# Where a unit's spread softmax shift is written: the bank of the preceding unit's column sums instead of spare columns of its PV banks

## The chip, the cores and the metric

The kernel runs on one core of a Trainium2 chip. The metric is the time of one execution on the device in microseconds, as the median of several runs; lower is better. Besides the timed runs there is one execution that the hardware profiler recorded. The engines are PE (matrix products), DVE (vector), ACT (scalar functions), POOL (GpSimd) and SP, which here only issues transfers. Matrix products are written to eight PSUM banks, each 512 float32 wide on 128 partitions; everything else is in SBUF.

## The reference, cut to what matters

Attention with normalised q and k, and behind it a two-layer product with a leaky ReLU:

```python
# q, k, v: (8, 12, 448, 64)
q_n, k_n = rmsnorm(q, g_q), rmsnorm(k, g_k)
scores = q_n @ k_n.transpose(0, 1, 3, 2) / sqrt(64)
attn = exp(scores - scores.max(-1)); attn = attn / attn.sum(-1)
x = (attn @ v).transpose(0, 2, 1, 3).reshape(8 * 448, 768)
h = x @ w_in                    # (3584, 2048)
out = maximum(0.01 * h, h) @ w_out   # (3584, 768)
```

The softmax needs no exact row maximum. Any shift that is the same for all keys of a row leaves the result as it is, as long as the exponentials stay in range. The kernel uses one shift for a whole unit.

## The kernel before, in words

**Units.** A unit is four heads of one batch: 3 units for each of 8 batches, 24 in all, u = 0 to 23. The four heads lie as two (r) on the halves of the partitions and two (a) in the two banks of a pair. The 448 tokens are 7 steps of 64.

**One unit.** `load` brings q and k in (SP's queue), two units to four ahead. `prep_sq` (ACT), `prep_ssq` (DVE, L186), `prep_rinv` (ACT) and `prep_norm` (DVE, L198) normalise them into `n16`; `prep_trd` transposes it by a transfer, and `prep_g` (DVE, L182) puts the gains on q. `score` (PE, L228) makes the transposed scores of one step in a pair of banks, and `ex` (ACT, L243) takes their exponential, `et`, with the unit's shift `eb` as bias. `pv` (PE, L400) multiplies with v over all 7 steps into two PV banks. `zcol` (PE, L337) makes the column sums of the exponentials in the first 224 columns of one more bank, `zc`.

**The shift.** `shift_max` takes the maximum over the scores of step 0 for each partition (DVE, L257) and puts the 128 values on the diagonal of a matrix, `dg` (L259). `shift_mm` brings them to all partitions: ones times `dg` on PE (L271), the maximum along the row (DVE, L274), and `eb` = 1 minus that (L284). Each PV bank has 64 spare columns behind its 448, and the product is written there in two halves, for units 4 to 23. Units 1 and 2 use spare columns of their own score banks, units 0 and 3 a free bank (L279).

**Copy and division.** `pv_out` copies the two PV banks to SBUF, `x32` (DVE at L350 for units 3 to 6, ACT at L352 for units 7 to 22), and `drop` gives the banks back. `zcol_ln` (ACT, L358) takes the logarithm of the sums and gives their bank back, `zcol_inv` (L363) takes exp of minus that, and four transfers (SP's queue, L368) spread the result over the partitions as `rz`. `xmul_pool` multiplies `x32` and `rz` into `xt` (L378): on POOL for units 7, 8, 11, 13, 14, 17, 19, 20 and 21, on DVE for the others (`xmul_sb`).

**The order.** All of it is written out by hand. The loop goes over u = 3 to 23 and four quarters d. For a narrow unit (`narrow`: u = 3 to 22) quarter 0 of the next one is recorded as follows:

```python
qk(u, (0,)); shift_max(u); flush()
pv_slot(u - 1); zcol(u - 1); shift_mm(u); pv_out(u - 1)
ex(u, 2); zcol_ln(u - 1)
```

Each engine works through its instructions in this order; semaphores make it wait where data or a bank require it. Waits are put in by the framework from the regions that instructions touch. `zcol_inv` follows as a job of quarter 0, `xmul_pool` in quarter 1. From u = 5 on (`tripled`) the score steps are recorded as 0, then 1 to 3 in quarter 1, then 4 to 6 in quarter 3.

**What lies between.** `fill` takes pieces of the two-layer product from `queue`, as many for each quarter as the strings of `PLAN` say, and puts a job behind each. `moe1` is the first layer (PE, L422; leaky ReLU on ACT, L416). The second layer is `moe2` (L468) and `seven` (L521), which makes a block product out of seven smaller ones: DVE makes sums of blocks of `gt` in `sa` (`s1` to `s4`: L502, L505, L508, L511), PE multiplies, and DVE adds the results to an output tile (L528, L543). Work that DVE or ACT does on a piece's result is put off by `later` until `flush`. The last two batches have the first layer in seven products too (`late1`, L655).

**Banks.** `aux` hands out a single bank and `slot` a pair, the one that has been free for longest within the rules; `drop` gives back. `banks` is one tile, so that all products have the name `banks` in the profile.

Of the kernel before, what the change touches and what calls it, by code (L numbers as in the profile page):

```python
# [8 lines left out]
FP32 = mybir.dt.float32  # L9
FP16 = mybir.dt.float16  # L10
AF = mybir.ActivationFunctionType
ALU = mybir.AluOpType
AXL = mybir.AxisListType
# [5 lines left out]
def kernel(  # L19
# [11 lines left out]
    nc = tc.nc  # L31

    B, H, S, D = q.shape
    QH = 4
    NS = 7
    P = 128
# [11 lines left out]
    small = ctx.enter_context(tc.tile_pool(name="small", bufs=2))  # L48
# [39 lines left out]
    def drop(tile_):  # L88
        for i in range(8):
            if tile_ is single[i]:  # L90
                assert i not in free
                free.append(i)
                return
        x = [i for i in range(4) if tile_ is double[i]][0]
        assert 2 * x not in free and 2 * x + 1 not in free
        free.extend((2 * x, 2 * x + 1))
# [9 lines left out]
    onesp = cst.tile([P, P], FP16)  # L106
# [32 lines left out]
    st = {}  # L139
# [121 lines left out]
    def shift_bank(u):  # L261
        st[u]["pb"] = aux()

    def shift_mm(u):
        s = st[u]
        peak = s["spare"][:, 510:511]
        own = s.get("own")
        if own is not None or u > 0 and "pslot" in st[u - 1]:
            pb = (st[u - 1]["pslot"] if own is None else own)[:, :, S:S + 64]
            for x in range(2):  # L270
                nc.tensor.matmul(pb[:, x], onesp, s["dg"][:, 64 * x:64 * x + 64], start=True, stop=True)  # L271
            if own is not None:
                peak = small.tile([P, 1], FP32, tag="peak", name="peak")
            nc.vector.tensor_reduce(peak, pb, axis=AXL.XY, op=ALU.max)  # L274
        else:
            if "pb" not in s:
                shift_bank(u)
            pb = s["pb"]
            nc.tensor.matmul(pb[:, 0:P], onesp, s["dg"], start=True, stop=True)  # L279
            nc.vector.tensor_reduce(peak, pb[:, 0:P], axis=AXL.X, op=ALU.max)  # L280
            if u >= 3:
                drop(pb)
        s["eb"] = small.tile([P, 1], FP32, tag="eb", name="eb")
        nc.vector.tensor_scalar(s["eb"], peak, -1.0, DELTA, op0=ALU.mult, op1=ALU.add)  # L284
# [550 lines left out]
    with tc.manual_schedule():  # L835
# [54 lines left out]
        shift_bank(0)  # L890
        warm(18, st[0]["pb"])
        shift_mm(0)
        drop(st[0]["pb"])
        prep_ssq(1)
# [47 lines left out]
        warm(4, wb)  # L942
        drop(wb)
        shift_mm(1)
        prep_ssq(2)
        ex(1)
# [29 lines left out]
        ex(1)  # L976
        warm_edge(16, st[0]["pv"][1])
        shift_mm(2)
        qk(1, (6,))
        ex(1)  # L980
# [203 lines left out]
```

## Time and profile before

| what | value |
|---|---|
| median of 3 runs | 409.88 us (409.75 to 410.16) |
| profiled execution | 409.67 us, its span 407.9 us |
| PE busy | 396.9 us, 97% of the span |
| DVE, ACT, POOL busy | 307.1, 300.6, 72.9 us |
| matmul of the shift, L271 | 44 instructions, 128x64, the first at 19.4 us, the last at 347.9 us |
| maximum over it, L274 | 22 instructions, 20 of them for units 4 to 23, 300 ns each (median) |
| copy of the PV banks by ACT, L352 | 16 instructions, 905 ns each (median) |

The profiled execution took 409.67 us, of which 407.9 us lie between its first and its last instruction. Times within it are counted from the first instruction. A line such as L352 is a line of the kernel before. Engine and letter q (SPq) mean that the engine's sequencer issued a transfer or waited. PE's matmuls are pipelined: they start closer together than they last, so distances are read from start to start.

### The profile page before, as it was taken

The numbers are of one execution on the slowest core, as the hardware profiler recorded it, in microseconds if no ns is written. First come the engines' busy times: TensorE is split into PE (matmuls) and PEld (weight loads), VectorE is DVE, ScalarE is ACT, GpSimd is POOL, SyncE is SP. The second block draws the span as 40 slices with busy tenths as digits, with TensorE's granted clock in tenths as the row PEclk, the third lists the DMA queues.
The fourth block names the chain that finished last, engine by engine and source line by source line (L and its number), as shares of the span: only waits on it lengthen the run. The fifth ranks groups of instructions, "written<-read, shape, count | busy, mean of one in ns | idle before, by whom it ended". The sixth has DMA issues, their size and how long they took to land.

```text
span 407.9 us, 9571 instructions
## 1 busy us (share of the span) xinstructions
PE 396.9 (97%) x3896; PEld 224.9 (55%) x3896; DVE 307.1 (75%) x481; ACT 300.6 (74%) x474; POOL 72.9 (18%) x86
## 2 busy tenths in 40 slices
PE   8999999999999999999999999999999999999996
PEld 7665454544455544555455544554455557559963
DVE  5887999959879665867679766777579888567672
ACT  5998877787978599778878689867996667743600
POOL 1887431200020200020021200021011202000000
PEclk9999999999999999999999999999999999999999
DMA  6999999898664984677664894776752560022023
GB/s 199 277 240 249 240 234 248 212 189 185 164 159 85 251 227 73 178 198 163 164 145 78 230 223 103 195 181 142 170 100 47 124 151 18 16 71 79 2 55 99
DMA packets 72526, 62.87 MB, mean 154 GB/s; under 512 B 36388, under 2 KB 67620, under 8 KB 72484
## 3 DMA queue, kind: packets, MB, share of 16 engines
q1 hardware_dynamic: 61888, 50.08, 46.8%
q0 software_dynamic: 10272, 11.80, 18.4%
q8 instruction: 30, 0.49, 0.5%
q10 hardware_dynamic: 324, 0.39, 0.3%
q14 instruction: 12, 0.10, 0.1%
HBM read 45.61 MB, written 11.01 MB: 139 GB/s over the span
## 4 chain that ended last, share of the span: by engine, by line
PE 80%; ACT 3%; DVE 3%; issue 2%; DMA 1%; SPq 1%; ACTq 0%; DVEq 0%
PE banks L422 27%; PE banks L521 23%; PE banks L228 8%; PE banks L655 6%; PE banks L400 6%; PE banks L468 6%; PE banks L337 3%; ACT et L243 1%; DMA rq<-in_q_dram 1%; SPq L368 1%; PE banks L271 1%; ACT gt L416 1%; DVE banks L257 1%; ACT sq L175 0%; PE banks L210 0%
## 5 line engine op out<-in xcount | busy, mean ns | idle before, releaser
L243 ACT ACTIVATE et<-banks,eb 128x896 f16<-128x896 f32 x168 | 161.4, 1015 | 28.9 <-PE banks L228 18.3
L422 PE MATMUL banks<-xt,win 128*128 128x448 f16 x612 | 122.4, 353 | 1.0 <-DVE xt L378 1.0
L422 PEld LDWEIGHTS <-win 128*128 128x128 f16 x612 | 57.3, 98 | 57.2 <-issue 8.0
L416 ACT ACTIVATE gt<-banks 128x448 f16<-128x448 f32 x104 | 56.4, 563 | 5.1 <-PE banks L422 3.9
L186 DVE TENSOR_REDUCE ssq<-sq 128x14 f32<-128x896 f32 (+2 forms) x49 | 50.3, 1057 | 0.7 <-ACT sq L175 0.7
L228 PE MATMUL banks<-qkT 64*64 64x448 f16 x672 | 49.3, 361 | 1.5 <-DVE qkT L810 0.8
L521 PEld LDWEIGHTS <-sa 128*128 128x128 f16 x352 | 33.4, 98 | 24.6 <-issue 3.6
L521 PE MATMUL banks<-tw,sa 128*128 128x384 f16 x264 | 46.9, 326 | 0.1
L528 DVE TENSOR_TENSOR ost<-banks,ost 128x384 f32<-128x384 f32 x55 | 30.4, 552 | 16.3 <-PE banks L521 14.3
L257 DVE TENSOR_REDUCE banks<-banks 128x1 f32<-128x896 f32 x24 | 26.3, 1097 | 14.2 <-PE banks L228 10.6
L400 PE MATMUL banks<-et,vt 64*64 64x448 f16 x672 | 36.9, 349 | 0.0
L521 PEld LDWEIGHTS <-gt 128*128 128x128 f16 x264 | 25.5, 98 | 18.7 <-issue 2.2
L468 PE MATMUL banks<-wout,gt 128*128 128x384 f16 x192 | 33.7, 327 | 0.0
L198 DVE TENSOR_TENSOR n<-rq,rinv 128x896 f16<-128x896 f32 (+2 forms) x25 | 31.0, 1241 | 3.1 <-ACT rinv L192 3.1
L228 PEld LDWEIGHTS <-qkT 64*64 64x64 f16 x672 | 16.9, 105 | 29.5 <-issue 22.5
L521 PE MATMUL banks<-wout,gt 128*128 128x384 f16 x176 | 32.4, 327 | 0.0
L290 POOL COPY gate_t<-qkT 128x1 f16<-128x1 f16 x16 | 4.8, 299 | 153.5 <-DMA qkT<-n 153.5
L378 POOL TENSOR_TENSOR xt<-x,rz 128x896 f16<-128x896 f32 x9 | 19.0, 2109 | 72.7 <-DMA rz<-zs 67.0
L352 ACT COPY x<-banks 128x896 f32<-128x896 f32 x16 | 14.5, 906 | 21.5 <-DVE banks L274 21.5
L198 DVE TENSOR_TENSOR n<-rk,rinv 128x896 f16<-128x896 f32 (+2 forms) x26 | 26.1, 1011 | 0.0
L400 PEld LDWEIGHTS <-vt 64*64 64x64 f16 x672 | 20.0, 107 | 10.0
L468 PEld LDWEIGHTS <-gt 128*128 128x128 f16 x192 | 17.8, 98 | 13.7 <-issue 2.9
(106 smaller groups left out, 484.7 us busy)
## 6 DMA issues: line engine op xcount, KB each, us to landing
rq<-in_q_dram SPq DMA_DIRECT2D x24, 448.0 KB, 4.8
rk<-in_k_dram SPq DMA_DIRECT2D x24, 448.0 KB, 5.3
out_dram<-ost SPq DMA_DIRECT2D x52, 192.0 KB, 3.4
rz<-zs SPq DMA_DIRECT2D x80, 112.0 KB, 2.8
vt<-in_v_dram POOLq DMA_DIRECT2D x24, 224.0 KB, 4.5
win<-in_moe_w_in_dram POOLq DMA_DIRECT2D x8, 384.0 KB, 14.9
wout<-in_moe_w_out_dram POOLq DMA_DIRECT2D x2, 1536.0 KB, 28.6
out_dram<-ost SPq DMA_DIRECT2D x4, 96.0 KB, 2.1
```

The costliest lines, as they stand in the source:

```text
L186: nc.vector.tensor_reduce(buf(u, "ssq")[:, ti, :, c[0]:c[1]], buf(u, f"sq{ti}")[:, :, c[0]:c[1]], axis=AXL.X, op=ALU.add)
L198: nc.vector.tensor_tensor(buf(u, "n16")[:, ti, c[0]:c[1]].rearrange("p s a d -> p a s d"), src[:, :, c[0]:c[1]], buf(u, "rinv")[:, ti, :, ...
L228: nc.tensor.matmul(banks[a][64 * r:64 * r + 64, 0:S].rearrange("p (t x) -> p t x", t=NS), kT(u, r, a, t), qT(u, r, a), start=True, stop=True)
L243: nc.scalar.activation(s["et"][:, t], sT[:, :, 0:S], AF.Exp, bias=s["eb"], scale=1.0)
L257: nc.vector.tensor_reduce(s["spare"][:, 511:512], sT[:, :, 0:S], axis=AXL.XY, op=ALU.max)
L400: nc.tensor.matmul(s["pv"][r][64 * a:64 * a + 64, 0:S], vts[u % NV][64 * r:64 * r + 64, a, t], s["et"][64 * r:64 * r + 64, t, a], start=(t ...
L416: nc.scalar.activation(dst, src, AF.Prelu, bias=0.0, scale=1.0, alpha=0.01)
L422: nc.tensor.matmul(hps[:, 0:S], win16[:, kt // 2, kt % 2, ts(ft, P)], xt[:, kt // 2, kt % 2], start=(kt == 0), stop=(kt == KT - 1))
L468: nc.tensor.matmul(op2[:, 0:HC], gt[:, ft, ds(col(t), P)], wout16[:, ft, ds(HC * half, HC)], start=(i == 0), stop=(i == FT - 1))
L521: nc.tensor.matmul(bank[:, 0:HC], a[:, f], b[:, f], start=(first and f == 0), stop=(f == HF - 1), skip_group_check=not first)
L528: nc.vector.tensor_tensor(dst, g[name][:, 0:HC], src, op=ALU.add)
L655: nc.tensor.matmul(bank[:, HX * i:HX * i + HX].rearrange("p (t x) -> p t x", t=NS), w, x[:, kt], start=start, stop=(kt == HK - 1), skip_gr ...
```

## The change

For units 4 to 23 the product of ones and `dg` is written in one piece of 128 columns into the bank `zc` of the preceding unit, at columns 256 to 383, behind the column sums in columns 0 to 223. Before, it was written in two pieces of 64 columns into the spare columns of the two PV banks of that unit. The maximum reads the new place. Units 0 to 3 keep their places. Nothing else is edited; lines behind the edit move by 3.

```diff
         own = s.get("own")
-        if own is not None or u > 0 and "pslot" in st[u - 1]:
-            pb = (st[u - 1]["pslot"] if own is None else own)[:, :, S:S + 64]
+        if own is not None:
+            pb = own[:, :, S:S + 64]
             for x in range(2):
                 nc.tensor.matmul(pb[:, x], onesp, s["dg"][:, 64 * x:64 * x + 64], start=True, stop=True)
-            if own is not None:
-                peak = small.tile([P, 1], FP32, tag="peak", name="peak")
+            peak = small.tile([P, 1], FP32, tag="peak", name="peak")
             nc.vector.tensor_reduce(peak, pb, axis=AXL.XY, op=ALU.max)
+        elif u > 0 and "zc" in st[u - 1]:
+            pb = st[u - 1]["zc"][:, 2 * P:3 * P]
+            nc.tensor.matmul(pb, onesp, s["dg"], start=True, stop=True)
+            nc.vector.tensor_reduce(peak, pb, axis=AXL.X, op=ALU.max)
         else:
```

## The prediction

> **What bounds the kernel now.** I read the busy shares first, then the waits, then the chain of work and the timeline around the places it pointed to. The page says that PE is the wall:
>
> ```profile
> PE 396.9 (97%) x3896; PEld 224.9 (55%) x3896; DVE 307.1 (75%) x481; ACT 300.6 (74%) x474; POOL 72.9 (18%) x86
> PE 80%; ACT 3%; DVE 3%; issue 2%; DMA 1%; SPq 1%; ACTq 0%; DVEq 0%
> ```
>
> The granted clock is 9 tenths or more in every slice. So the time can only change by what PE executes and by the moments at which PE waits. Among the waits one belongs to the lines of this change:
>
> ```profile
> ACT x L352 <- DVE banks L274: 21.5, 13, 3.3
> ```
>
> ACT's copy of the PV result (L352, 16 units) waits 21.5 us in all, 13 times, for the maximum over the spread shift (L274) that DVE takes from the same two banks. ACT is not the wall, so this is no sum to subtract; it says who will run earlier. I looked for what that sets going in unit 20's first half, around the copy for unit 19 (timeline: start, us, engine, line, operation, count; in brackets the idle time ahead):
>
> ```profile
> 297.37 3.57 PE L422 MATMUL banks<-xt,win 128*128 128x448 f16 x18
> 298.01 0.91 ACT L352 COPY x<-banks 128x896 f32<-128x896 f32 x1 [0.72 <-DVE banks L274]
> 298.01 0.16 DVE L284 TENSOR_SCALAR eb<-banks 128x1 f32<-128x1 f32 x1
> 298.81 1.01 ACT L243 ACTIVATE et<-banks,eb 128x896 f16<-128x896 f32 x1
> 300.37 0.41 ACT L363 ACTIVATE zs<-zs 128x224 f32<-128x224 f32 x1
> 300.80 2.48 SPq L368 DMA_DIRECT2D rz<-zs  x4
> 304.63 0.42 DVE L502 TENSOR_TENSOR sa<-gt 128x512 f16<-128x512 f16 x1 [0.17 <-ACT gt L416]
> 305.09 0.42 DVE L505 TENSOR_TENSOR sa<-sa,gt 128x512 f16<-128x512 f16 x1
> 305.14 2.32 POOL L378 TENSOR_TENSOR xt<-x,rz 128x896 f16<-128x896 f32 x1 [6.04 <-DMA rz<-zs]
> 305.16 1.46 PE L521 MATMUL banks<-tw,sa 128*128 128x384 f16 x8
> 305.90 1.84 DVE L508 TENSOR_TENSOR sa<-gt 128x512 f16<-128x512 f16 x1
> 308.00 0.55 DVE L528 TENSOR_TENSOR ost<-banks,ost 128x384 f32<-128x384 f32 x1
> ```
>
> Read it downwards: copy, exponential, reciprocal of the sums (L363), four broadcasting DMAs, POOL's product (L378). And read L508: the same shape takes 0.42 us elsewhere, here 1.84 us, ending 0.28 us after POOL's product. While POOL runs L378, a DVE sum of two SBUF tiles stands still (L198 too, 2.42 instead of 1.08 us). L528 and L543, with an operand in PSUM, keep their 0.55 us beside POOL.
>
> **The change part by part.** In the changed build PE's order is the old one less 20 matmuls, and no wait of PE changes. The copy at L352 now waits for the last PV matmul, not for DVE.
>
> *Matmuls.* Twenty pairs of 128x64 become single 128x128. A pair goes from 172.34 to the next matmul at 172.41: 0.068 us. The 128x128 form stands once in this trace (L279), 40.41 to 40.46: 0.056 us. 20 x 0.012 = 0.24 us less, on PE's path. An unknown is the new bank: the shift now follows the column sums (L337) into their own bank. At worst it waits until they drain, 0.26 us for one L337 against the 0.19 us that already lies between them: 20 x 0.07 = 1.4 us more. L422's six matmuls into one bank follow each other without loss, each 0.19 us; that is the nearest row, so I take 0 and keep 1.4 for the range.
>
> *Same-bank order.* The row is the 21.5 us: two readers of one bank were put one after the other. The Trainium skill (PSUM — Partial Sum Buffer, "PSUM bank collisions raise a hardware error") says why: two engines must not touch one bank and quadrant at once, whatever columns they use. That speaks against the change, since the sums' bank has a reader of its own, ACT's logarithm at L358. In unit 17 it starts at 268.36, L274 ends at 266.63, and the exponential between them needs L274's result anyhow: nothing is added.
>
> *ACT earlier.* The copy (0.91 us) now runs before eb is ready, so the exponential follows eb. In unit 19 the PV matmuls end at 296.88, ACT's work before at 297.28, the copy then at 298.2; eb ends at 298.17, and the exponential follows it by 0.09 us where eb is its releaser (81.31 to 81.40): 298.26 instead of 298.81, 0.55 us earlier. The same sum gives 0.55 to 0.6 us for 13 of the 16 units, and 0.1 or less for units 7, 10 and 16, where ACT itself was late. L358, L363, the DMAs and L378 all move with it.
>
> *What PE gains by that.* Only where it waits today. From the chain (start, us, what):
>
> ```profile
> 175.18 0.90 PE banks L228 x12
> 268.25 0.90 PE banks L228 x12
> ```
>
> And from the timeline behind the second:
>
> ```profile
> 273.56 2.07 POOL L378 TENSOR_TENSOR xt<-x,rz 128x896 f16<-128x896 f32 x1 [7.05 <-DMA rz<-zs]
> 276.51 0.55 DVE L528 TENSOR_TENSOR ost<-banks,ost 128x384 f32<-128x384 f32 x1
> 277.11 1.46 PE L521 MATMUL banks<-tw,gt 128*128 128x384 f16 x8 [0.55 <-DVE ost L528]
> ```
>
> Twelve score matmuls take 0.69 us elsewhere; at 175.18 and 268.25 they wait for banks that an exponential and L358 give back: 2 x 0.21 = 0.42 us gained. At 277.11 PE waits 0.55 us for L528, late because L198 (2.85 us) stood behind POOL from 273.73. Unit 17's DMAs can go 0.41 us earlier (SP's stores end at 268.75); PE is by then 0.21 earlier itself: 0.20 us gained. All gains: 0.24 + 0.42 + 0.20 = 0.86 us.
>
> *What PE loses.* Unit 19's product moves from 305.14 to 304.59, ahead of L502 at 304.63. Alone it takes 2.08 us: until 306.67. L502 ends 0.28 later, 306.95, L505 0.46 after that, 307.41. L505's tile feeds the fifth matmul of the group at 305.16, due at 305.16 + 4 x 0.163 = 305.81; it starts at 307.46 at the earliest: 1.6 us lost. The bounds are 0 (POOL after L505 has started) and 1.7. Should L502 start first by some 0.04 us, it depends on whether POOL gets in behind it. The row: POOL's one-column copy at 265.24 took 0.62 us and ended 0.05 after an L508, while the L511 queued directly behind had been issued; so POOL gets in between.
>
> A rule behind it: the Trainium skill (SBUF — State Buffer, "Who interferes with whom") makes this an exclusive lock that goes to whoever issues first, for the whole instruction. It does not say that a waiting POOL comes before the next queued DVE instruction; if DVE kept it until L505 were through, this term would be 0 and the sum below -0.26.
>
> Unit 13 has the same place in the order, a little later:
>
> ```profile
> 212.12 0.41 DVE L508 TENSOR_TENSOR sa<-gt 128x512 f16<-128x512 f16 x1
> 212.45 0.42 DVE L511 TENSOR_TENSOR sa<-gt,sa 128x512 f16<-128x512 f16 x1
> 212.69 2.12 POOL L378 TENSOR_TENSOR xt<-x,rz 128x896 f16<-128x896 f32 x1 [8.02 <-DMA rz<-zs]
> 212.87 0.56 DVE L528 TENSOR_TENSOR ost<-banks,ost 128x384 f32<-128x384 f32 x1
> ```
>
> Moved by 0.55 it meets L508 at 212.14, gets in by 212.53 and ends at 214.6; L511 ends at 214.9, L528 at 215.4. PE's group behind the next scores, due at 214.82, needs L528's bank: 0.6 us lost (0 if the DMAs land after 212.4; the last took 3.6 us today, the others 2.3 to 2.5). In unit 7, third at this place, L505 starts at 118.11 and POOL moves only 0.1, to 118.37: at most 0.05. In units 8, 11, 14, 20 and 21 no sum of two SBUF tiles lies in the 0.6 us ahead of L378; there L198 only gets shorter, which PE does not wait for.
>
> *Sum:* -0.86 + 1.6 + 0.6 + 0.05 - 0.05 (PE's present wait at 308.60, which goes) = +1.34 us on the profiled execution's 409.67, so 411.0; on the median, 0.21 above it, 409.88 + 1.34 = 411.2.
>
> **The rivals.**
> 1. *Gains alone, faster.* POOL's product does not get ahead of L505 and L511: DVE keeps the lock, or the DMAs don't land earlier. -0.86: 409.0. For it: the margins are 0.04 to 0.4 us. Against it: unit 19's DMAs land evenly, 2.3 us after each issue. It decides at a product that starts 0.05 us earlier than now, or not.
> 2. *Unit 19 collides, unit 13 doesn't.* -0.86 + 1.6 - 0.05: 410.6. For it: unit 13's slow last DMA.
> 3. *ACT's head start doesn't arrive* (a wait for the previous x32 or zs takes its place): -0.24 only, 409.6. Against it: both buffers are free long before. Unit 13 alone colliding gives the same: 409.6.
> 4. *More than forecast*: the bank drain of 1.4 us, or collisions without the gains, about 412 to 412.6.
>
> **How the numbers follow.** Both collide: 0.42, about 411.2. Unit 19 alone: 0.20. Nothing arrives or unit 13 alone: 0.15. Gains alone: 0.15. More: 0.08. A measurement here can tell some 0.2% (0.82 us) from no change, so the bounds are 409.06 and 410.70. Faster takes the gains alone and a little for gains that I sized too small: 0.17. Slower takes both collisions but a tail, the case of more, and a third of unit 19 alone, which ends near the bound: 0.55. The rest, 0.28, is the same. The range runs from rival 1's 409.0 to 412.0, leaving out the largest case of more and what lies below rival 1. The first case's own range is 410.6 to 411.9.
>
> **What would show it.** After: 20 matmuls fewer; L352 waiting for PE or nobody; exponentials some 0.55 us nearer to the score matmuls; POOL's product ahead of L502 in unit 19, with L502 or L505 over 1.8 us and PE idle some 1.6 us after it; L511 over 2 us in unit 13; 0.69 in place of 0.90 us in units 11 and 17. I am wrong if L352 starts no earlier, if PE is idle at a place that isn't named here, or if the last L337 to the shift exceeds 0.19 us.

## The result and the profile after

The changed kernel takes 413.05 us (median of 8 runs, 410.46 to 414.66) against 409.97 us for the kernel before on the same chip (8 runs, 408.81 to 410.94): a ratio of 1.0075 [1.0046, 1.0104]. It is slower by 3.1 us; forecast were 1.3 us. Its profiled execution took 413.97 us with a span of 412.2 us, 4.3 us more than the profiled execution before. In what follows lines are those of the kernel they stand in: behind the edit, the new kernel's numbers are higher by 3. The four sums of DVE are called `s1` to `s4` (L502, L505, L508, L511 before; L505, L508, L511, L514 now).

The page first: busy time and instructions of each engine, then the shares of the chain that ended last.

```profile
PE 397.0 (96%) x3876; PEld 224.6 (54%) x3876; DVE 310.0 (75%) x481; ACT 302.8 (73%) x474; POOL 72.9 (18%) x86
PE 74%; DVE 9%; DMA 3%; SPq 1%; issue 1%; ACT 1%; DVEq 0%; ACTq 0%
```

PE has its 20 matmuls less and is as busy as before, 397.0 us, in a longer span: all that was lost is idle time. DVE's share of the chain went from 3% to 9%. POOL works as long as before, to the tenth; DVE is 2.9 us busier without one instruction more, so some of its instructions take longer.

The waits name them (engine, tile and line that waited, what for: us in all, times, longest):

```profile
ACT x L355 <- PE banks L403: 4.3, 10, 2.0
PE banks L524 <- DVE sa L508: 4.3, 3, 1.5
```

The copy waits for the last PV matmul, 4.3 us in place of 21.5 us for DVE's maximum: the change does what it says. And PE has a wait that it didn't have, three times some 1.45 us, for `s2`. The timeline at unit 19's product shows the place that the forecast had named (start, us, engine, line, operation, tiles; in brackets the idle time ahead and what ended it):

```profile
298.76 0.95 ACT L355 COPY x<-banks 128x896 f32<-128x896 f32 x1
299.00 3.57 PE L425 MATMUL banks<-xt,win 128*128 128x448 f16 x18
299.64 0.16 DVE L287 TENSOR_SCALAR eb<-banks 128x1 f32<-128x1 f32 x1
299.83 1.01 ACT L243 ACTIVATE et<-banks,eb 128x896 f16<-128x896 f32 x1
301.40 0.40 ACT L366 ACTIVATE zs<-zs 128x224 f32<-128x224 f32 x1
301.83 2.48 SPq L371 DMA_DIRECT2D rz<-zs  x4
306.18 2.07 POOL L381 TENSOR_TENSOR xt<-x,rz 128x896 f16<-128x896 f32 x1 [6.07 <-DMA rz<-zs]
306.25 2.28 DVE L505 TENSOR_TENSOR sa<-gt 128x512 f16<-128x512 f16 x1 [0.28 <-ACT gt L419]
306.77 0.81 PE L524 MATMUL banks<-tw,sa 128*128 128x384 f16 x4
308.57 0.42 DVE L508 TENSOR_TENSOR sa<-sa,gt 128x512 f16<-128x512 f16 x1
309.05 0.82 PE L524 MATMUL banks<-tw,sa 128*128 128x384 f16 x4 [1.46 <-DVE sa L508]
```

Counted from the shift's matmul (297.30 before, 298.94 now), the copy starts 0.89 us sooner, the exponential 0.62, the transfers 0.61 and POOL's product 0.60. That puts the product 0.07 us ahead of `s1`, not 0.51 us behind it. `s1` takes 2.28 us, not 0.42, and ends 0.28 us after the product; `s2`, whose tile the fifth matmul of PE's group reads, ends at 308.99, and PE goes on at 309.05. The sequence is the one forecast, line by line.

Units 13 and 7, of the same timeline (unit 13 first):

```profile
211.87 0.43 DVE L505 TENSOR_TENSOR sa<-gt 128x512 f16<-128x512 f16 x1 [0.28 <-ACT gt L419]
211.93 2.30 POOL L381 TENSOR_TENSOR xt<-x,rz 128x896 f16<-128x896 f32 x1 [5.13 <-ACT gt L419]
212.33 2.18 DVE L508 TENSOR_TENSOR sa<-sa,gt 128x512 f16<-128x512 f16 x1
214.57 0.82 PE L524 MATMUL banks<-tw,sa 128*128 128x384 f16 x4 [1.36 <-DVE sa L508]
...
117.78 2.07 POOL L381 TENSOR_TENSOR xt<-x,rz 128x896 f16<-128x896 f32 x1 [5.34 <-DMA rz<-zs]
117.79 2.34 DVE L508 TENSOR_TENSOR sa<-sa,gt 128x512 f16<-128x512 f16 x1
120.18 0.82 PE L524 MATMUL banks<-tw,sa 128*128 128x384 f16 x4 [1.52 <-DVE sa L508]
```

In unit 13 `s1` had begun 0.06 us earlier and kept its 0.43 us; the product waited it out (2.30 us, not 2.07) and came before `s2`, which was next on DVE. In unit 7 the product began 0.01 us ahead of `s2`: nearly a tie. Each costs PE about what it costs in unit 19. In the kernel before, unit 7's product came 0.36 us behind `s2` (L505), which kept its 0.42 us:

```profile
118.11 0.42 DVE L505 TENSOR_TENSOR sa<-sa,gt 128x512 f16<-128x512 f16 x1
118.47 2.08 POOL L378 TENSOR_TENSOR xt<-x,rz 128x896 f16<-128x896 f32 x1 [5.73 <-DMA rz<-zs]
```

To place every loss I set the start of each PE matmul of one profile against the same matmul of the other. The distance changes only in steps:

| time before, us | step, us | place |
|---|---|---|
| up to 91.75 | -0.30 | start of the program, and a wait for an `rz` of a unit that DVE multiplies |
| 118.82 | +1.67 | unit 7: product ahead of `s2` |
| 121.69 | -0.12 | unit 7: a short wait of before is shorter |
| 175.4, 176.0 | -0.20 | unit 11: scores |
| 212.02 | +1.51 | unit 13: product ahead of `s2` |
| 268.5, 269.1 | -0.21 | unit 17: scores |
| 277.11 | -0.71 | unit 17: the wait for L528 is gone |
| 305.81 | +1.61 | unit 19: product ahead of `s1` |
| 339.22 | +0.72 | unit 21: product ahead of the sum of exponentials |
| 347.97 | +0.30 | unit 22: a sum on DVE and the `dg` behind it are late |
| end | +4.26 | sum of all, with -0.01 of small ones |

Unit 21 was not in the forecast. Timeline of the new kernel there:

```profile
340.04 2.08 POOL L381 TENSOR_TENSOR xt<-x,rz 128x896 f16<-128x896 f32 x1 [14.03 <-DVE ea L325]
340.07 2.53 DVE L325 TENSOR_TENSOR ea<-ea,et 128x896 f16<-128x896 f16 x1
342.52 0.61 DVE L677 COPY u<-banks 128x448 f32<-128x448 f32 x1
343.19 0.73 PE L658 MATMUL banks<-xs,ws 128*128 128x224 f16 x6 [0.59 <-DVE u L677]
```

The sum of exponentials (`ea`, 0.62 us by itself) adds two SBUF tiles. Before, it ended at 337.48, 0.65 us ahead of the product; now the product starts 0.03 us ahead of it, and the copy behind the sum, which frees a bank that PE needs, is late. The kernel before:

```profile
336.85 0.63 DVE L322 TENSOR_TENSOR ea<-ea,et 128x896 f16<-128x896 f16 x1
338.13 2.09 POOL L378 TENSOR_TENSOR xt<-x,rz 128x896 f16<-128x896 f32 x1 [14.87 <-DMA rz<-zs]
```

The step of 0.30 us at 347.97 is another matter. There a DVE sum (L668 before, L671 now) begins 0.37 us later, counted from PE, and `dg` and the shift of unit 23 follow it. The same step stands in the profile of all but three (below), where unit 21 has no collision, and not in that of the gate on `s2`, where it has one. What holds the sum up the profiles don't show.

The score matmuls of units 11 and 17 gained what they were to gain: in the chain (start, us, what) they now take 0.69 us like all others, not 0.90.

```profile
176.42 0.69 PE banks L228 x12
270.81 0.69 PE banks L228 x12
```

### The profile page after: what moved, and what is told of

Read it like the earlier page. It is cut to its first block, busy times and chain, and to the rows that moved or that the text cites. A ratio compares the mean times of both kernels' runs of the same rounds, so it can differ in the third digit from the quotient of the medians.

```text
span 412.2 us, 9531 instructions
## 1 busy us (share of the span) xinstructions
PE 397.0 (96%) x3876; PEld 224.6 (54%) x3876; DVE 310.0 (75%) x481; ACT 302.8 (73%) x474; POOL 72.9 (18%) x86
## 4 chain that ended last, share of the span: by engine, by line
PE 74%; DVE 9%; DMA 3%; SPq 1%; issue 1%; ACT 1%; DVEq 0%; ACTq 0%
PE banks L425 25%; PE banks L524 23%; PE banks L228 7%; PE banks L658 6%; PE banks L403 6%; PE banks L471 4%; PE banks L340 2%; DMA rz<-zs 2%; SPq L371 1%; DVE sa L508 1%; DMA rq<-in_q_dram 1%; DVE banks L257 1%; DVE sa L505 1%; DVE n L198 1%; PE banks L276 1%
## 5 line engine op out<-in xcount | busy, mean ns | idle before, releaser
L531 DVE TENSOR_TENSOR ost<-banks,ost 128x384 f32<-128x384 f32 x55 | 30.5, 554 | 19.0 <-PE banks L524 16.3
L293 POOL COPY gate_t<-qkT 128x1 f16<-128x1 f16 x16 | 3.8, 239 | 155.1 <-DMA qkT<-n 155.1
L198 DVE TENSOR_TENSOR n<-rq,rinv 128x896 f16<-128x896 f32 (+2 forms) x25 | 27.4, 1098 | 2.0 <-ACT rinv L192 1.9
L198 DVE TENSOR_TENSOR n<-rk,rinv 128x896 f16<-128x896 f32 (+2 forms) x26 | 27.6, 1067 | 0.0
L559 ACT COPY ost<-banks 128x384 f32<-128x384 f32 x11 | 5.3, 480 | 27.5 <-PE banks L524 27.5
```

The source lines that it names most:

```text
L198: nc.vector.tensor_tensor(buf(u, "n16")[:, ti, c[0]:c[1]].rearrange("p s a d -> p a s d"), src[:, :, c[0]:c[1]], buf(u, "rinv")[:, ti, :, ...
L531: nc.vector.tensor_tensor(dst, g[name][:, 0:HC], src, op=ALU.add)
```

## The experiments

The theory: the new bank costs nothing; POOL's product, earlier by the copy's head start, comes ahead of a DVE sum of two SBUF tiles that PE waits for, in units 7, 13 and 19. The rivals: the shift's new place costs something by itself (a bank that must drain), or the earlier copy disturbs PE in another way than through POOL. The first four kernels were compared with the kernel before at 410.24 us (20 runs), the last four at 410.04 us (23 runs). Steps of PE are found as above, against the profile before, at the times of before.

**The wait put back, the bank kept.** The maximum is written into the old PV banks, so that the copy waits for DVE again.

```diff
             pb = st[u - 1]["zc"][:, 2 * P:3 * P]
+            peak = st[u - 1]["pslot"][:, 0, 510:511]
             nc.tensor.matmul(pb, onesp, s["dg"], start=True, stop=True)
```

> The change with ACT's old wait put back: the maximum over the shift is written into a spare column of the PV banks, so that the copy to x32 waits for DVE again (for eb, 0.2 us later than before the change); the product stays in the bank of the column sums. Theory 1 (ACT's head start moves POOL's product ahead of DVE's sums of SBUF tiles): the products of units 7, 13 and 19 fall back to their old places or 0.2 us behind, no DVE sum at L505 over 0.5 us, PE loses nothing there; 409.7 to 410.4 us. Rival (the new bank itself costs PE time, 3 us over 20 units): stays at 412 to 414 us.

412.63 us (6 runs), ratio 1.0068 [1.0051, 1.0084]: not the theory's time, but one in the rival's range. In the profile, though, the three losses are gone, and PE has no step at any shift. Instead it has steps of 0.22 to 0.27 us at the score matmuls of seven units (1.7 us together). The timeline at unit 11 shows why:

```profile
174.05 0.16 DVE L288 TENSOR_SCALAR eb<-banks 128x1 f32<-128x1 f32 x1
174.30 0.91 ACT L356 COPY x<-banks 128x896 f32<-128x896 f32 x1 [2.10 <-DVE eb L288]
175.10 1.01 ACT L243 ACTIVATE et<-banks,eb 128x896 f16<-128x896 f32 x1
176.16 0.63 PE L228 MATMUL banks<-qkT 64*64 64x448 f16 x8 [0.21 <-ACT et L243]
```

As foreseen, the copy waits for `eb` (L288), not only for the maximum ahead of it, and starts 0.25 us after `eb`, where in the kernel before the two start together. What the expectation missed is that PE feels it: the exponential is later by that, and PE waits for its bank. The profiled execution was the shortest of the six, 411.44 us, and these steps explain it; the 1.2 us that the median has on top are in no profile. (In units 13 and 19 the product starts only 0.05 us behind `s2` here.) So the time of this run decides nothing between theory and rival. Its one profile shows no loss at the new bank and none at the three sums, and how thin ACT's margin is at these scores.

**The products held back.** In units 7, 13 and 19 POOL reads one column of `s4` first, so that its product can't begin ahead of `s4`; in the changed kernel and, for the price of that, in the kernel before.

```diff
         nc.vector.tensor_tensor(sa[:, 3, x], gblock(tt[0], 1)[:, x], sa[:, 1, x], op=ALU.subtract)
+        if held and x.start == 4:
+            nc.gpsimd.tensor_copy(gate_t, sa[:, 3, HF - 1, P - 1:P])
+            xmul_pool(held.pop())
...
-                    xmul_pool(u - 1)
+                    if u - 1 in (7, 13, 19):
+                        held.append(u - 1)
+                    else:
+                        xmul_pool(u - 1)
```

> The change, with POOL's products of units 7, 13 and 19 held until DVE's last sum of that place (L511 of the kernel before) is done, by a one-column copy on POOL ahead of them; ACT's head start stays. Theory 1: the three waits of PE of 1.5 to 1.7 us are gone and the gains (1.2 us by the two traces) stay; 408.7 us, up to 409.8 if unit 21's product still collides with the sum of exponentials. Rival (the bank, or traffic that starts earlier): 412 to 414 us, PE idle elsewhere.

> The kernel before with the same gate on POOL's products of units 7, 13 and 19. It tells what the gate does by itself. Theory 1: DVE's L508 of 1.9 us in units 7 and 19 shrinks to 0.4 us, which PE hardly waited for (0.05 to 0.13 us each): 409.6 to 410.1 us, so that what e2 has over it is the change's own gain, about 1.2 us. Rival (the gate itself is what helps, change or not): e3 as far below 409.97 us as e2.

The changed kernel takes 411.25 us with it (12 runs), 1.0025 [1.0007, 1.0042], where it had 1.0075 without; the kernel before takes 411.48 us with it (9 runs), 1.0031 [1.0018, 1.0045]. Both expected less (408.7 to 409.8 and 409.6 to 410.1 us). The steps of 1.5 to 1.7 us are gone from the first. The gate doesn't help the kernel before, so the rival that it would help either kernel falls. The gate has a price in both: three steps of 0.46 to 0.48 us, because the held product now lies on L198. Timeline of the kernel before with the gate, unit 7:

```profile
120.15 2.08 POOL L379 TENSOR_TENSOR xt<-x,rz 128x896 f16<-128x896 f32 x1
120.26 2.91 DVE L198 TENSOR_TENSOR n<-rq,rinv 128x896 f16<-128x896 f32 x1
126.75 0.29 DVE L259 TENSOR_TENSOR dg<-ident,banks 128x128 f16<-128x128 f16 x1
127.09 0.22 PE L271 MATMUL banks<-dg,onesp 128*128 128x64 f16 x2 [0.42 <-DVE dg L259]
```

L198 takes 2.91 us, not 1.08; DVE doesn't catch up until the next unit's `dg`, and PE waits 0.42 us for it. The forecast had passed over L198 as one that PE does not wait for; made longer at this place, it is waited for. With the same gate the two kernels are 0.2 us apart, where gains of about 1 us were expected; the changed kernel had steps of +0.57 and +0.41 us in units 11 and 14 in this profile, of which more below.

**Early without the new bank.** The kernel before, with its shift in the PV banks; only for units 7, 13 and 19 the copy is put behind the logarithm and the reciprocal on ACT, so that these come earlier.

```diff
-                            pv_out(u - 1)
+                            if u in (8, 14, 20):
+                                drop(st[u - 1]["pslot"])
+                            else:
+                                pv_out(u - 1)
...
-                            job(zcol_inv, u - 1)
+                            if u in (8, 14, 20):
+                                jobs.append(lambda: (zcol_inv(u - 1), pv_out(u - 1, False)))
+                            else:
+                                job(zcol_inv, u - 1)
```

> The kernel before, shift in the PV banks, but with ACT's copy of units 7, 13 and 19 placed behind the reciprocal of the sums, so that the four transfers and POOL's product go about 0.9 us earlier in these three units alone. Theory 1: DVE sums (L502, L505 or L508) stand behind POOL there for about 2 us and PE idles 0.3 to 1.6 us in each; 412 to 414 us, of which up to 0.25 us in each unit is the later copy, seen at the score matmuls behind it. Rival (the bank costs): the bank is the old one, 409.9 to 410.7 us.

415.24 us (4 runs), 1.0124 [1.0106, 1.0142], 1.2 us above the range expected, as each collision cost nearly the most that was expected of it. Steps: +1.69, +1.58 and +1.44 us at the three sums (and 0.20 to 0.22 us at three groups of scores). Timeline, unit 7:

```profile
117.47 2.07 POOL L379 TENSOR_TENSOR xt<-x,rz 128x896 f16<-128x896 f32 x1 [5.10 <-DMA rz<-zs]
117.53 2.30 DVE L503 TENSOR_TENSOR sa<-gt 128x512 f16<-128x512 f16 x1
119.86 0.42 DVE L506 TENSOR_TENSOR sa<-sa,gt 128x512 f16<-128x512 f16 x1
120.34 0.82 PE L522 MATMUL banks<-tw,sa 128*128 128x384 f16 x4 [1.48 <-DVE sa L506]
```

This is the old bank, the old two matmuls, and the same loss: being early is enough.

**Held back less.** The gate reads a column of `s2` in place of `s4`, which lets the product begin 8.56 us behind the shift's matmul.

```diff
         nc.vector.tensor_tensor(sa[:, 1, x], sa[:, 0, x], gblock(tt[0], 0)[:, x], op=ALU.subtract)
+        if held and x.start == 4:
+            nc.gpsimd.tensor_copy(gate_t, sa[:, 1, HF - 1, P - 1:P])
+            xmul_pool(held.pop())
```

> The change with POOL's products of units 7, 13 and 19 held only until L505 (the sum that PE needs next) is done, not until L511. In e2 and e3 the later gate pushed the product onto L198 and cost 0.48 us at the next unit's shift, three times. Theory 1: the product lies where it lay before the change, behind L505 and on L508; no PE wait of 1.5 us, no 0.48 us either; the change's gains stay: 409.0 to 409.8 us beside 410.2 for the kernel before. Rival (any early product costs, it is only moved on): 411 to 413 us.

412.17 us (6 runs), 1.0050 [1.0031, 1.0070]. The expectation failed. The three losses are gone, but POOL's gate and product come ahead of `s3`, which takes 2.33 us, `s4` and L528 behind it are late, and PE loses 0.40, 0.53 and 0.50 us there; units 14 and 21 lose 0.37 and 0.61 us. So a product that starts 8.56 us behind the shift's matmul costs 0.4 to 0.5 us, and one at 9.70 us (the gate on `s4`) as much at L198, while those of the kernel before, at 7.84, 8.16 and 9.17 us, cost PE some 0.1 us at most: its places were free ones, and neither gate hits one.

**The change for all units but three, and for three alone.** The old place is kept for u = 8, 14 and 20 (whose shift goes with the copies of units 7, 13 and 19), or for all others.

```diff
-        elif u > 0 and "zc" in st[u - 1]:
+        if own is None and u > 0 and "zc" in st[u - 1] and u not in (8, 14, 20):
             pb = st[u - 1]["zc"][:, 2 * P:3 * P]
```

> The change for all units except 8, 14 and 20, whose shift stays in the PV banks of units 7, 13 and 19, so that the copies and products of these three keep their old times. Theory 1: the three collisions are gone, the gains in units 11 and 17 (0.4 to 1.1 us) and of 17 matmuls (0.2 us) stay, unit 21 may lose up to 1: 409.0 to 409.9 us. Rival (the new bank, or the head start in general, costs): 17 of 20 parts of the loss stay, 412 to 413 us.

> The change for units 8, 14 and 20 alone, the counterpart of e6. Theory 1: nearly the whole loss is here: PE waits 1.4 to 1.7 us at the sums of units 7, 13 and 19, or less where a product happens to come later; 412.5 to 415 us. Rival: 3 of 20 parts of the loss, 410.3 to 410.8 us.

All but three: 409.84 us (11 runs), 0.9990 [0.9976, 1.0003]. Three alone: 413.08 us (5 runs), 1.0071 [1.0058, 1.0084]. Both lie within what was expected. By the medians the three units carry the whole loss of the full change, 3.0 of 3.1 us (the intervals reach 0.5 and 1.2 us to either side). And the rival of the new bank falls: with 17 of the 20 shifts in it, the kernel is no slower than before. Unit 19 in the profile of all but three, where the copy waits as before:

```profile
303.56 0.42 DVE L506 TENSOR_TENSOR sa<-gt 128x512 f16<-128x512 f16 x1 [0.17 <-ACT gt L420]
304.02 0.42 DVE L509 TENSOR_TENSOR sa<-sa,gt 128x512 f16<-128x512 f16 x1
304.08 2.31 POOL L382 TENSOR_TENSOR xt<-x,rz 128x896 f16<-128x896 f32 x1 [6.09 <-DMA rz<-zs]
304.83 1.84 DVE L512 TENSOR_TENSOR sa<-gt 128x512 f16<-128x512 f16 x1
```

The product begins 0.06 us after `s2` (L509), `s2` keeps its 0.42 us, and only `s3` pays. The other 17 units bring no gain that can be told from nothing.

In the profile of three alone, units 13 and 19 lose 1.62 and 1.61 us, unit 7 nothing:

```profile
117.66 0.42 DVE L509 TENSOR_TENSOR sa<-sa,gt 128x512 f16<-128x512 f16 x1
117.83 2.20 POOL L382 TENSOR_TENSOR xt<-x,rz 128x896 f16<-128x896 f32 x1 [5.29 <-DMA rz<-zs]
```

Here the product came 0.17 us after `s2`; in the full change 0.01 us before it.

**POOL writes, but doesn't read.** For units 7, 13 and 19 of the changed kernel the product is left out; POOL copies one column of `rz`, so that it starts when the product would, and fills `xt` with zeros.

```diff
-                    xmul_pool(u - 1)
+                    if u - 1 in (7, 13, 19):
+                        nc.gpsimd.tensor_copy(gate_t, st[u - 1]["rz"][:, 1, S - 1:S])
+                        nc.gpsimd.memset(xts[(u - 1) // NQ][:, (u - 1) % NQ], 0.0)
+                    else:
+                        xmul_pool(u - 1)
```

> The change, with POOL's products of units 7, 13 and 19 left out: POOL fills their place in xt with zeros instead, once the last transfer of rz has landed, so that it writes SBUF but reads next to nothing. If it is POOL's reading that holds up DVE's sums of two SBUF tiles, L502 and L505 keep their 0.42 us beside the fill and PE waits nowhere there: 408.8 to 409.8 us. If any POOL instruction holds them up, L505 takes the length of the fill, and PE loses that.

409.63 us (10 runs), 0.999 [0.998, 1.000], within what was expected if it is POOL's reading. Timeline, unit 19:

```profile
303.46 0.83 POOL L1101 MEMSET xt<- 128x896 f16 x1
303.49 0.42 DVE L505 TENSOR_TENSOR sa<-gt 128x512 f16<-128x512 f16 x1 [0.28 <-ACT gt L419]
303.94 0.42 DVE L508 TENSOR_TENSOR sa<-sa,gt 128x512 f16<-128x512 f16 x1
304.01 0.81 PE L524 MATMUL banks<-tw,sa 128*128 128x384 f16 x4
```

POOL begins 0.03 us ahead of `s1`, lies on `s1` and `s2` for 0.83 us, and neither takes longer; so it is in unit 13 (fill at 210.70, `s1` from 210.64, `s2` from 211.10, 0.42 us each). In unit 7 the fill came at 118.70, after `s2` had ended, where in other profiles a product costs nothing either; so units 13 and 19 are the test. PE has no step in the three units. With bank, matmuls and early ACT all as in the changed kernel, the loss goes when POOL reads nothing there. The fill is shorter than the product, but `s1` lies wholly under it, so it did not wait for POOL. The Trainium skill (SBUF — State Buffer, "Who interferes with whom") says that a DVE instruction with two SBUF inputs contends with a GpSimd instruction that reads SBUF, not with one that only writes it. This run agrees with the second half (0.42 us beside the fill), the changed kernel's profile with the first (2.28 us beside the product).

## Why the prediction was right or wrong

**The threshold.** Measured from the start of the shift's matmul on PE, `s1` starts 7.31 to 7.33 us and `s2` 7.77 to 7.79 us behind it in units 7, 13 and 19, where nothing holds them up; in the two kernels whose copy lies later (marked *) `s1` starts after 7.57 to 7.59 us and `s2` after 8.03 to 8.05 us. The start of POOL's product, on the same scale, sorts the profiles:

| profile | unit 7 | unit 13 | unit 19 | PE's loss, us |
|---|---|---|---|---|
| before | 8.16 | 9.17 | 7.84 | none |
| after | 7.77 | 7.38 | 7.24 | 1.67, 1.51, 1.61 |
| early, old bank * | 7.53 | 7.79 | 7.27 | 1.69, 1.58, 1.44 |
| wait put back * | 8.44 | 8.09 | 8.10 | none at the sums |
| all but three | 7.90 | 7.85 | 7.85 | none |
| three alone | 7.94 | 7.26 | 7.24 | none, 1.62, 1.61 |
| held behind `s2` | 8.56 | 8.57 | 8.56 | 0.40, 0.53, 0.50, behind `s3` |
| held behind `s4` | 9.70 | 9.70 | 9.70 | none at the sums, 0.47 each behind L198 |

Ahead of `s2` of its own kernel: 1.4 to 1.7 us; behind it: none of that loss. (The 7.79 of the early kernel lost because `s1` itself was late there, `s2` with it at 8.05.) Unit 19's margin in the kernel before is 0.05 us.

**Right.** The copy's wait goes, the copy is early, POOL gets ahead: rival 3 falls, and rival 1 with it. Unit 19: forecast 1.6, measured 1.61 us. A product that finds DVE at work goes in before DVE's next instruction, on which the range had hung: unit 13 shows it. The scores of units 11 and 17: forecast 0.42, measured 0.41 us. The bank: the shift follows the last column sum by 0.19 us as before (but for unit 7, 0.64 us in both kernels, and unit 23, 0.51 us behind the late `dg`), and the next matmul follows the shift as it did; taken as 0, it is 0.

**Wrong: two collisions too small.** The sum missed because the terms "unit 13: 0.6" and "unit 7: at most 0.05" measured 1.51 and 1.67 us. Both failed at one step, which took the landing of the last `rz` transfer from one profile as fixed. For unit 13 the forecast moved the product by 0.55 us from 212.69 and let the last transfer take its 3.6 us, though it had noted 2.3 to 2.5 for the other three (with the copy at its old place, the last took 3.63, 3.96 and 2.31 us in three profiles); it took 2.44 us, so the product met `s1` and went in ahead of `s2`, where the forecast had it meet `s3` and go in ahead of `s4`. For unit 7 it moved the product by 0.1 us; the last transfer went out 0.12 us sooner and landed in 2.32 us, not 2.60, which makes 0.4 us together; some 0.02 us less would have been free. From issue to landing this transfer took between 2.3 and 4.3 us over the profiles of this study, at units 7, 11, 13 and 14. The forecast's clause for unit 13, 0 if the transfers land later, looked at the one side of that only.

**Wrong: unit 21 left out.** "No sum of two SBUF tiles in the 0.6 us ahead" was true by 0.05 us: the sum of exponentials ended 0.65 us ahead of the product. The product moved 1.3 us relative to PE. The first transfer went out 0.66 us sooner; the last went out 1.4 us sooner, because a pause of 0.8 us between the second and the third on SP's queue was gone, and it landed 2.3 us after its issue in both profiles. The collision cost 0.72 us, and as much in the profile with POOL's fill, where unit 21 is as in the changed kernel. By its own sign (PE idle at a place not named) the forecast was wrong here: it had let this product move by no more than 0.6 us.

**Wrong: the matmuls.** Forecast 0.24 us for 20 merged matmuls. The pair took 0.068 us from start to start, the single one takes 0.066 to 0.067: 0.03 us in all. The row that I used, L279 at 0.056 us (one of two in the trace, not the only one), didn't stand behind column sums as these do. Where the shift itself comes late, 0.51 to 0.64 us behind the last column sum, the next matmul follows it after 0.055 to 0.057 us too, the pair (unit 7 before) as well as the single one (units 7 and 23 now). So the distance hangs on what went ahead, not on the form alone.

**Right in sign for a wrong reason: unit 17's wait.** Forecast -0.20 us because the transfers would go earlier; measured -0.71. But the transfers hardly went earlier: 0.25 us counted from the shift, not 0.41, and only 0.04 us counted from PE, which is itself 0.21 us earlier behind the scores. The last one landed 0.74 us later, counted from PE (3.09 us after its issue, not 2.30):

```profile
276.07 1.08 DVE L198 TENSOR_TENSOR n<-rq,rinv 128x896 f16<-128x896 f32 x1
276.64 2.46 POOL L381 TENSOR_TENSOR xt<-x,rz 128x896 f16<-128x896 f32 x1 [7.98 <-DMA rz<-zs]
277.07 0.55 DVE L531 TENSOR_TENSOR ost<-banks,ost 128x384 f32<-128x384 f32 x1
277.54 2.51 DVE L198 TENSOR_TENSOR n<-rk,rinv 128x896 f16<-128x896 f32 x1
```

The product came behind the first L198 instead of ahead of it, L531 was in time, and the second L198 paid, for which PE doesn't wait. The same luck is in two more profiles (all but three, POOL's fill) but not in those of the two gates on the changed kernel, where the copy is as early. So I don't count it as a sure gain of the change. Nor do I lay to the change the -0.30 us of the start, which differs as much among the profiles without it. The losses of 0.3 to 0.6 us that single profiles show in units 11 and 14 come with a late last transfer: 4.0 to 4.3 us, against 2.3 to 3.0 in the two compared kernels; in the kernel before with a gate, 3.5 us and 0.3 us lost in unit 14.

Whether the head start brings these about can only be counted. In five profiles units 11, 14, 17 and 21 have it (after, both gates on the changed kernel, all but three, POOL's fill), in the other five they don't. Unit 17 gains its 0.71 us in three of the five with it and in none without. Unit 21 loses 0.6 to 0.7 us in three against none, unit 14 0.3 to 0.4 us in three against one, unit 11 0.57 us in two against none. So gains and losses both come with the head start more often than without it; together with the 0.41 us of the scores they about cancel over the five. Five profiles are too few to tell a rate.

**What stays open.** Two collisions of 1.6 us make 3.2, and the medians say 3.1 for the full change and 3.0 for the three units alone. How often unit 7 is the third, and how often unit 21 loses its 0.7 us, is open, as the changed kernel has one profile, of an execution 0.9 us above its median; that these two make the wide spread of the new kernel's times, 4.2 us against 2.1, fits and is not shown. Whether a version that keeps the old place also for units 11, 14 and 21 would be faster than the kernel before is open. No kernel here is faster than the one before by more than can be told.

## What to carry to other kernels

Before a wait is taken away on an engine that is not the bound, list what will run earlier because of it, and for each such instruction that shares something with another engine, the margin to the next instruction on that engine. Where the margin is smaller than the spread of the transfer that releases it, the term has two values and neither is "today's": take the landing from several instances, not from the one row beside it. An early arrival can be worse than a late one, and where the time of arrival can't be set, the order should be.

## What the runs showed of the hardware

POOL's product (2.07 us, two SBUF inputs) blocks a DVE sum of two SBUF tiles that begins 0.01 to 0.07 us after it to the product's end and beyond: 2.28 to 2.34 us, not 0.42, ending 0.28 to 0.29 us after POOL. The other way round DVE isn't hurt: a sum that began 0.06 us earlier keeps its 0.43 us, POOL's product then lasts 2.30 us, and, what I had inferred from one row only, POOL gets in before the DVE instruction that stands next. DVE's work with an operand in PSUM (L531, L546) keeps its 0.55 us beside POOL's product, and DVE's sums keep their 0.42 us beside a POOL fill that only writes (0.83 us).

A small transfer is no constant: the fourth of four `rz` transfers landed 2.3 to 4.3 us after its issue, with the same shapes and nearly the same neighbours. Against margins of 0.01 to 0.07 us, that can decide whether 1.6 us are lost: in unit 7 the product lost by 0.01 us in the changed kernel and was clear by 0.17 us in the profile of three alone, with the same edit there.
